# All layer-norm factor steps on GpSimd, two tiles projected in float32, and a rearranged start, in a fused attention and MLP-mixer kernel

## The chip, the cores and the metric

The kernel runs on one core of a Trainium2 chip. The time is the device time of one execution in microseconds (us). Five engines run beside each other, each with its own list of instructions that it works off in order: TensorE (PE, matmuls, with its weight loads as PEld), VectorE (DVE), ScalarE (ACT), GpSimd (POOL) and SyncE (SP), which here issues every DMA. They wait for each other only through semaphores.

## The reference, cut to what matters

```python
xn = layernorm(x)                                   # 2048 rows of 512, float32
qkv = xn @ wqkv                                     # 512 x 1536; 32 heads of 16
# row s attends to rows s, s-2, ..., s-14 (8 keys, dilation 2); s < 0 masked
o = softmax(q.k * 16**-0.5) @ v;  s = o @ wo
y = layernorm(xn)                                   # a second norm, on the first one's result
h = gelu_tanh(y @ w1 + b1)                          # 512 -> 1376
g = silu(h @ w2 + b2)                               # 1376 -> 512
return x + s * g
```

## The kernel before, in words

**Tiles.** The 2048 rows are split into two classes of 1024 (even and odd rows, `c` = 0 and 1), each in 8 tiles `i` of 128 rows by 512. A unit is one class and one block of 8 heads (`hb` = 0 to 3), so there are 8 units, class 0 first. A unit has its projection (`qkv`: 8 tiles, each 12 matmuls of 384 columns) and its attention (`attention`, nearly all on VectorE). The MLP has 4 chunks of 512 rows and 11 blocks `f` of 128 hidden units; one block is 12 matmuls of 512 columns in `mlp1` and 12 in `mlp2`. The output projection is `wo_first` for class 0 and `wo_last` for class 1.

**Precision.** A float32 operand is held as a float16 half `hi` and a remainder `lo`, and a product is three float16 matmuls (hi hi, lo hi, hi lo). Weights are scaled by a power of two first, which needs the sum of their squares: `prep_q` for `wqkv`, and the blocks around `sumsq` and `split` for `w1`, `w2` and `wo`. A sum of squares runs on ScalarE, is totalled over partitions by a small matmul with the matrix `fours` (`total`), and VectorE works out the scale (`half_exp`, `up`, `down`). ScalarE or VectorE then makes `hi`, and VectorE makes `lo`.

**Layer norm.** `ln0` norms class 0. Per group of tiles: `stats` (mean and variance, VectorE), then `factors`. The two norms are folded into one: `rb` is the factor of the row, `cT` a second one that is put in when the projection is evicted (`cs` is `cT` times the weights' inverse scale). In `factors` the two powers run on GpSimd (L512 for `rb`, L519 for `cT`) and the steps between them on VectorE (L504, L508, L515 to L518). The normed tile `y` is made by VectorE (L564) or, for groups whose first tile is in `ACT_Y`, by ScalarE (`y_act`, L531 and L534). TensorE transposes it (L571), ScalarE casts it to `hi` (L581), VectorE makes `lo` (L582). `ln1` does the same later for class 1, in one group of 8.

**Order.** `Plan` takes all operations with an estimated duration and a priority, and places them one by one; what it places fixes each engine's list. A projection may start when the readers of the buffer `U` that it will be evicted into are placed (`after` in `qkv`). Small rings of buffers (`Ring`) set how far one engine can run ahead: two PSUM banks `ps`, two `mh`, four `z`, two for scores `L`. `WAKE0` and `WAKE` are matmuls on constants (L1044) that keep TensorE busy before there is data.

**Loads.** `LOADS` is the order of the first DMAs: tile 2 of `x`, the two halves of the first `wqkv` block (`"q0"`, `"q2"`), tile 3, then tiles 0 and 1, 4 and 5, 6 and 7 in pairs; after them `w1`, the second `wqkv` block, and `w2`. Groups are normed in the order of `GROUPS`.

Of the kernel before, what the change touches and what calls it, by code (L numbers as in the profile page):

```python
# [18 lines left out]
P = 128  # L19
# [5 lines left out]
NI = 8  # L25
# [52 lines left out]
class Op:  # L78
    __slots__ = ("eng", "dur", "fn", "prio", "table", "bufs", "preds", "succs", "npred",
                 "ready", "nbytes", "n", "port", "rate", "issue", "tail")  # L80


class Plan:
# [9 lines left out]
    def add(self, eng, dur, fn, reads=(), writes=(), prio=None, table=None, nbytes=0,  # L93
            after=None, holds=(), port=False, rate=350e3, issue=0.55, tail=1.4):
# [15 lines left out]
        o.port, o.rate, o.issue, o.tail = port, rate, issue, tail  # L110
# [159 lines left out]
WAKE0 = 22  # L270
# [7 lines left out]

U1MH = 4
# [4 lines left out]
PURG, WURG = 0.14, 0.05  # L284
DVE1 = 1.0417e-3
# [5 lines left out]
def tile_mixer(ctx, tc, a_x, a_wqkv, a_wo, b_w1, b_b1, b_w2, out):  # L291
# [168 lines left out]
    def prep_q(hb):  # L460
        col = R_s.new()
        for k in range(0, KT, 2):
# [5 lines left out]
            act(768, go, [("stq", hb, k)], [(col, k), ("wqh", hb, k), ("wqh", hb, k + 1)],  # L468
# [25 lines left out]
    def factors(n, mv, mk, cdst, ckeys, bias=True, close=None, pp=None, **k):  # L494
# [9 lines left out]
        dve(n, lambda: nc.vector.tensor_scalar(p0b.t[:, 0:n], V(), (1.0 + EPS) / YS ** 2,  # L504
                                               EPS * EPS / YS ** 2, op0=ALU.mult, op1=ALU.add),
            mk, [p0b], **k)
        if bias:
            dve(n, lambda: nc.vector.tensor_scalar(p0b.t[:, 8:8 + n], mv()[:, 0:n, 0], -1.0, None,  # L508
                                                   op0=ALU.mult), mk, [(p0b, 1)], **k)
        if close:  # L510
            close()
        pool(0.42 + 0.14 * n, lambda: nc.gpsimd.tensor_tensor(  # L512
            rb.t[:, 0:n], p0b.t[:, 0:n], halves[:, 0:n], op=ALU.pow), [p0b], [(rb, 0)], prio=pp, port=False)
        with pl.fuse():
            dve(n, lambda: nc.vector.tensor_scalar(a0(), V(), EPS, None, op0=ALU.add), mk, [(A, 0)])  # L515
            dve(n, lambda: nc.vector.reciprocal(a1(), a0()), [(A, 0)], [(A, 1)])
            dve(n, lambda: nc.vector.tensor_tensor(a1(), a1(), V(), op=ALU.mult), [(A, 1)] + mk, [(A, 1)])
            dve(n, lambda: nc.vector.tensor_scalar(a1(), a1(), EPS, None, op0=ALU.add), [(A, 1)], [(A, 1)])  # L518
        pool(0.42 + 0.14 * n, lambda: nc.gpsimd.tensor_tensor(  # L519
            cdst, a1(), halves[:, 8:8 + n], op=ALU.pow), [(A, 1)], ckeys, port=False)  # L520
        return rb, p0b
# [6 lines left out]
    def y_act(x, rb, a, keys, y, *ykey):  # L528
        rb, p0b = rb
        with pl.fuse("act"):  # L530
            act(1, lambda: nc.scalar.activation(rb.t[:, 8 + a:9 + a], p0b.t[:, 8 + a:9 + a], AF.Identity,  # L531
                                                scale=rb.t[:, a:a + 1]),
                [(rb, 0), (p0b, 1)], [(rb, 1, a)])
            act(512, lambda: nc.scalar.activation(  # L534
                y(), x(), AF.Identity, bias=rb.t[:, 8 + a:9 + a], scale=rb.t[:, a:a + 1]),
                keys + [(rb, 0), (rb, 1, a)], list(ykey), aps=2)
# [701 lines left out]
```

## Time and profile before

| | |
|---|---|
| median of 3 executions | 424.58 us (423.83 to 424.82) |
| the profiled execution | 423.72 us, of which the span of the profile is 421.9 us |
| TensorE busy | 410.7 us (97%) |
| VectorE busy | 392.1 us (93%) |
| ScalarE busy | 216.0 us (51%) |
| GpSimd busy | 78.9 us (19%) |
| granted TensorE clock, mean | 0.99 of full speed |

A row of the timeline gives start, duration, engine, line of the kernel, operation, `out<-in` by tile names with shapes, a count of like instructions in a row, and in brackets the idle time before it with what ended it. A row of a table by stage gives, for a stretch of time, its length, the busy time of each engine with the number of instructions, the granted clock of TensorE, the share of the DMA engines and their rate. In a row of grouped instructions stand count, busy time, mean of one in ns, and the idle time before.

### The profile page before, as it was taken

How to read it: one execution, taken by the hardware profiler on the slowest of the kernel's cores; microseconds unless marked ns; L12 is line 12 of the kernel's file. 1: busy time of each engine (PE TensorE's matmuls, PEld its weight loads, DVE VectorE, ACT ScalarE, POOL GpSimd, SP SyncE). 2: the span in 40 equal slices, each digit the busy share in tenths (PEclk: the TensorE clock that was granted, in tenths of full speed). 3: DMA queues.
4: the chain of work that ended last, by engine and by line, in shares of the span. 5: the costliest groups of instructions: out<-in, count | busy, mean ns of one | idle time of the engine just before them, and what ended most of it. 6: DMA issues, size and time to landing. Idle time of an engine off the chain costs nothing.

```text
span 421.9 us, 5568 instructions
## 1 busy us (share of the span) xinstructions
PE 410.7 (97%) x2111; PEld 209.8 (50%) x2111; DVE 392.1 (93%) x402; ACT 216.0 (51%) x325; POOL 78.9 (19%) x119
## 2 busy tenths in 40 slices
PE   6899999999999999999999999999999999999995
PEld 4466544445644464446545644554445544444442
DVE  5967999999999999899999999999999999999953
ACT  5699984862478553942565361325122664263500
POOL 4310200001451052003400520052003400520031
PEclk8899999999999999999999999999999999999999
DMA  8964260120044047440362051114434344016132
GB/s 302 414 225 138 62 224 2 63 88 0 6 123 159 2 100 187 100 98 3 91 170 76 2 140 47 46 54 138 149 110 91 94 101 143 2 38 211 26 124 99
DMA packets 42650, 44.83 MB, mean 106 GB/s; under 512 B 27480, under 2 KB 27920, under 8 KB 42112
## 3 DMA queue, kind: packets, MB, share of 16 engines
q1 hardware_dynamic: 42624, 44.49, 34.7%
q8 instruction: 16, 0.26, 0.3%
q14 instruction: 10, 0.08, 0.1%
HBM read 23.53 MB, written 7.34 MB: 73 GB/s over the span
## 4 chain that ended last, share of the span: by engine, by line
DVE 46%; PE 39%; issue 8%; DMA 3%; POOL 2%; SPq 1%; ACT 1%; DVEq 0%; ACTq 0%
DVE prod L691 10%; PE z L945 10%; PE ps L632 9%; PE mh L900 9%; DVE L L694 8%; DVE prod L747 6%; DVE prod L742 5%; PE ps L817 5%; DVE h L923 2%; PE z L817 2%; PE mh L632 2%; POOL prod L771 2%; DVE w L437 2%; DVE bn L525 2%; DVE wq L485 1%
## 5 line engine op out<-in xcount | busy, mean ns | idle before, releaser
L900 PE MATMUL mh<-yT,w 128*128 128x512 f16 (+1 forms) x528 | 121.3, 379 | 0.7 <-ACT h L932 0.5
L632 PE MATMUL ps<-wq,yT 128*128 128x384 f16 x696 | 117.8, 328 | 0.5 <-DVE f L831 0.5
L945 PE MATMUL z<-w,h 128*128 128x512 f16 x480 | 111.6, 379 | 0.0
L632 PEld LDWEIGHTS <-yT 128*128 128x128 f16 x768 | 75.7, 99 | 51.5 <-issue 2.4
L900 PEld LDWEIGHTS <-w 128*128 128x128 f16 (+1 forms) x528 | 52.9, 100 | 61.8 <-issue 1.2
L945 PEld LDWEIGHTS <-h 128*128 128x128 f16 x480 | 47.0, 98 | 55.2
L691 DVE TENSOR_TENSOR prod<-U 128x2048 f32<-128x2048 f32 x32 | 73.1, 2291 | 1.3 <-DMA U<-U 0.2
L917 ACT ACTIVATE mh<-mh,b1T,hsc 128x512 f32<-128x512 f32 (+1 forms) x44 | 33.0, 749 | 79.9 <-PE mh L900 73.4
L694 DVE TENSOR_REDUCE L<-prod 128x128 f32<-128x2048 f32 x32 | 72.8, 2282 | 0.4
L648 ACT ACTIVATE U<-ps,cs 128x384 f32<-128x384 f32 x58 | 33.6, 579 | 67.6 <-PE ps L632 62.8
L747 DVE TENSOR_TENSOR prod<-L,U 128x2048 f32<-128x2048 f32 x28 | 63.4, 2284 | 0.2
L770 POOL COPY gate<-prod 1x1 f32<-1x1 f32 x21 | 4.4, 210 | 236.4 <-DVE prod L691 204.7
L742 DVE TENSOR_TENSOR prod<-prod,prod 128x2048 f32<-128x2048 f32 x16 | 36.5, 2281 | 0.0
L771 POOL TENSOR_TENSOR prod<-prod 128x1024 f32<-128x1024 f32 x14 | 32.9, 2351 | 0.0
L817 PEld LDWEIGHTS <-oT 128*128 128x128 f16 x189 | 18.5, 98 | 22.1
L920 ACT ACTIVATE h<-mh,hsc 128x512 f16<-128x512 f32 x40 | 27.4, 686 | 0.9
L817 PE MATMUL ps<-wo,oT 128*128 128x512 f16 x120 | 27.0, 379 | 0.0
L923 DVE SCALAR_TENSOR_TENSOR h<-mh,hsc,h 128x512 f16<-128x512 f32 x32 | 23.8, 743 | 1.1 <-ACT h L920 1.1
L730 ACT ACTIVATE o<-prod,osc 128x1024 f16<-128x1024 f32 (+1 forms) x9 | 9.5, 1052 | 15.1 <-POOL prod L771 10.5
L771 POOL TENSOR_TENSOR prod<-prod,prod 128x1024 f32<-128x1024 f32 x7 | 16.4, 2349 | 0.0
L917 ACT ACT_TABLE_LOAD x11 | 14.1, 1283 | 0.2
L632 PE MATMUL mh<-wq,yT 128*128 128x384 f16 x72 | 13.4, 330 | 0.0
(151 smaller groups left out, 340.5 us busy)
## 6 DMA issues: line engine op xcount, KB each, us to landing
f<-in_A_x_dram SPq DMA_DIRECT2D x31, 256.0 KB, 3.5
U<-U SPq DMA_DIRECT2D x16, 392.0 KB, 3.8
gd<-f SPq DMA_DIRECT2D x12, 256.0 KB, 2.0
oT<-in_B_w_dram SPq DMA_DIRECT2D x2, 1024.0 KB, 10.3
yT<-in_B_w_dram SPq DMA_DIRECT2D x2, 1024.0 KB, 12.8
f<-gd SPq DMA_DIRECT2D x8, 256.0 KB, 3.1
out_dram<-f SPq DMA_DIRECT2D x8, 256.0 KB, 2.0
out_dram<-U SPq DMA_DIRECT2D x7, 256.0 KB, 2.0
```

Of the source, the lines that this page charges most:

```text
L632: nc.tensor.matmul(b.t[:, 0:384], y[:, s, k, o:o + P], wq[:, hb, t, k], start=(n == 0), stop=(n == 11))
L648: act(384, lambda i=i, b=b: nc.scalar.activation(U3[:, i:i + 31:15, :], b.t[:, 0:384].rearrange("p (t e) -> p t e", t=3), AF.Identity, sca ...
L691: dve(2048, lambda p2=p2, g=g: nc.vector.tensor_tensor(p2(), q, slots(Ut, KH, 2 * g), op=ALU.mult), qk + [("kh", ub, 0), ("kh", ub, 1), (" ...
L694: dve(2048, lambda pr=pr, g=g: nc.vector.tensor_reduce(L3()[:, 2 * g:2 * g + 2], pr.t.rearrange("p (r f d) -> p r f d", r=2, d=DH), AX.X, ...
L742: dve(n, lambda: nc.vector.tensor_tensor(d(), a(), b(), op=ALU.add), keys, [dkey])
L747: dve(2048, lambda: nc.vector.tensor_tensor(pr.t.rearrange("p (r f d) -> p r f d", r=2, d=DH), L3()[:, 2 * g:2 * g + 2].rearrange("p r (f ...
L771: nc.gpsimd.tensor_tensor(x.t[:, 0:1024], x.t[:, 0:1024], y(), op=ALU.add)
L817: nc.tensor.matmul(b.t, oT[:, hb, i // 4, s, i % 4], wo[:, t, hb], start=(hb == 0 and n == 0), stop=(hb == last and n == 2))
L900: nc.tensor.matmul(b.t[0:M], w1[:, s, k, f * P:f * P + M], yT[ch][:, t, k], start=(n == 0), stop=(n == 11))
L917: act(512, lambda: nc.scalar.activation(b.t[0:M], b.t[0:M], AF.Gelu_apprx_tanh, bias=b1T[0:M, f:f + 1], scale=hsc[0:M, 1:2]), [b, ("b1T",) ...
L923: dve(512, lambda: nc.vector.scalar_tensor_tensor(lo()[0:M], b.t[0:M], hsc[0:M, 2:3], hi()[0:M], op0=ALU.mult, op1=ALU.subtract), [b, hk], ...
L945: nc.tensor.matmul(z.t, hl[s][0:K, t * P:(t + 1) * P], w2[0:K, w, f], start=(f == 0 and n == 0), stop=(f == NF - 1 and n == 2))
```

## The change

- `factors` runs wholly on GpSimd. The reciprocal of VectorE is gone: `cT` is now YS^-1 (var + eps)^-0.5 times `p0b` times `rb`. The bias of a tile that ScalarE norms (minus mean times factor) is made there too, one step per tile, and the small ScalarE step (L531) is gone. `cs` of unit 0 is made on GpSimd.
- Tiles 0 and 1 are normed singly, and tile 0's `y` is made on VectorE (`ACT_Y` without 0).
- Tiles 2 and 3 (`FP`) are projected for unit 0 in float32: ScalarE copies the transposed tile to SBUF in float32, TensorE multiplies it by the loaded, unscaled `wqkv` in 4 matmuls of 384 columns. Their float16 halves, which the later units and the MLP read, are made later than tile 1's (`later`).
- `LOADS` puts tile 3 between the two halves of the first `wqkv` block and loads tiles 0 and 1 by two DMAs. `prep_q(0)` gets a lower priority and is added after the first group.
- Four more matmuls on constants (`WAKE0`).
- For units 2 to 7 only the first tile's projection waits for the readers of `U`, for all of q, k and v, and is planned 3 us later (`QSLACK`); the other tiles wait only for a PSUM bank.
- Blocks 2 and 3 of the first MLP chunk use the `ps` banks (`AHEAD`); ScalarE makes the halves of `h` in the order of the blocks.
- The ring `lw` has 24 buffers for 8.

```diff
-GROUPS = [(2,), (3,), (0, 1), (4, 5), (6, 7)]
-LOADS = [(2, 1), "q0", "q2", (3, 1), (0, 2), (4, 2), (6, 2)]
-FP = ()
-ACT_Y = (0, 1, 4, 5)
+GROUPS = [(2,), (3,), (0,), (1,), (4, 5), (6, 7)]
+LOADS = [(2, 1), "q0", (3, 1), "q2", (0, 1), (1, 1), (4, 2), (6, 2)]
+FP = (2, 3)
+ACT_Y = (1, 4, 5)
...
-WAKE0 = 22
+WAKE0 = 26
+AHEAD = (2, 3)
+PQ0 = 0.35
+QSLACK = 3.0
...
     def factors(n, mv, mk, cdst, ckeys, bias=True, pp=None):
-        dve(n, lambda: nc.vector.tensor_scalar(p0b.t[:, 0:n], V(), (1.0 + EPS) / YS ** 2,
-                                               EPS * EPS / YS ** 2, op0=ALU.mult, op1=ALU.add),
-            mk, [p0b], **k)
+        small, power = 0.21, 0.42 + 0.14 * n
+        pool(small, lambda: nc.gpsimd.tensor_scalar(
+            p0b.t[:, 0:n], V(), (1.0 + EPS) / YS ** 2, EPS * EPS / YS ** 2, op0=ALU.mult, op1=ALU.add),
+            mk, [p0b], prio=pp, port=False)
+        pool(power, lambda: nc.gpsimd.tensor_tensor(
+            rb.t[:, 0:n], p0b.t[:, 0:n], halves[:, 0:n], op=ALU.pow), [p0b], [(rb, 0)], prio=pp, port=False)
         if bias:
-            dve(n, lambda: nc.vector.tensor_scalar(p0b.t[:, 8:8 + n], mv()[:, 0:n, 0], -1.0, None,
-                                                   op0=ALU.mult), mk, [(p0b, 1)], **k)
+            for a in range(n):
+                pool(small, lambda a=a: nc.gpsimd.tensor_scalar(
+                    rb.t[:, 8 + a:9 + a], mv()[:, a:a + 1, 0], rb.t[:, a:a + 1], -1.0, op0=ALU.mult, op1=ALU.mult),
+                    [mk[a], (rb, 0)], [(rb, 1, a)], prio=pp, port=False)
-        with pl.fuse():
-            dve(n, lambda: nc.vector.tensor_scalar(a0(), V(), EPS, None, op0=ALU.add), mk, [(A, 0)])
-            dve(n, lambda: nc.vector.reciprocal(a1(), a0()), [(A, 0)], [(A, 1)])
-            dve(n, lambda: nc.vector.tensor_tensor(a1(), a1(), V(), op=ALU.mult), [(A, 1)] + mk, [(A, 1)])
-            dve(n, lambda: nc.vector.tensor_scalar(a1(), a1(), EPS, None, op0=ALU.add), [(A, 1)], [(A, 1)])
-        pool(0.42 + 0.14 * n, lambda: nc.gpsimd.tensor_tensor(
-            cdst, a1(), halves[:, 8:8 + n], op=ALU.pow), [(A, 1)], ckeys, port=False)
+        pool(small, lambda: nc.gpsimd.tensor_scalar(
+            a0(), V(), EPS, YS ** -2, op0=ALU.add, op1=ALU.mult), mk, [(A, 0)], port=False)
+        pool(power, lambda: nc.gpsimd.tensor_tensor(a0(), a0(), halves[:, 0:n], op=ALU.pow),
+             [(A, 0)], [(A, 0)], port=False)
+        pool(small, lambda: nc.gpsimd.tensor_tensor(
+            a1(), p0b.t[:, 0:n], rb.t[:, 0:n], op=ALU.mult), [p0b, (rb, 0)], [(A, 1)], port=False)
+        pool(small, lambda: nc.gpsimd.tensor_tensor(cdst, a0(), a1(), op=ALU.mult), [(A, 0), (A, 1)], ckeys, port=False)
...
     def y_act(x, rb, a, keys, y, *ykey):
-        with pl.fuse("act"):
-            act(1, lambda: nc.scalar.activation(rb.t[:, 8 + a:9 + a], p0b.t[:, 8 + a:9 + a], AF.Identity,
-                                                scale=rb.t[:, a:a + 1]),
-                [(rb, 0), (p0b, 1)], [(rb, 1, a)])
...
     def ln0(ii, xs, xkeys):
-                yf = yF[i] = R_L.new()
+                yf = yF[i] = (R_L if i in (2, 3) else R_f).new()
...
+            (later.append if i in FP else apply)(halves16)
...
     def qkv(c, hb, u):
-                   after=pl.users([b] + [("v", ub, i)]))
+                   after=pl.users([b] + [(x, ub, j) for x in "qkv" for j in range(NI)] if n == 0 else [b]),
+                   slack=QSLACK if u > 1 and n == 0 else 0.0)
...
     def mlp1(ch, f):
-        b = R_mh.new()
+        b = (R_ps if ch == 0 and f in AHEAD else R_mh).new()
...
-                                                  scale=hsc[0:M, 2:3]), [b], [hk])
+                                                  scale=hsc[0:M, 2:3]),
+                [b] + [("hseq", NF * ch + f - 1)] * (NF * ch + f > 0), [hk, ("hseq", NF * ch + f)])
...
-    pl.prio = 0.05
-    prep_q(0)
     pl.prio = 0.1
     for p in groups:
+        if p == groups[1]:
+            with prio(PQ0):
+                prep_q(0)
         pl.prio += 0.1
         ln0(p, [xk[i][0] for i in p], [xk[i][1] for i in p])
+    for f in later:
+        f()
```

In the planned lists this moves the following. VectorE has 37 instructions fewer: 32 small ones less before the MLP, one `y` more, and 6 small ones less in `ln1`. ScalarE has 12 of L531 less, one `y` less and two float32 copies more. GpSimd has 2 powers and 45 small steps more. On TensorE 24 float16 matmuls of 384 columns become 8 in float32, and 4 on constants are added. TensorE's list now has the transposes of tiles 3, 0 and 1 between the float32 matmuls of tiles 2 and 3, and the total of `prep_q(0)` behind the transposes of tile 3. In the units 2 and 3 two tiles of the projection come earlier, among MLP blocks. In `wo_last` the first three head blocks of tiles 0 to 3 (36 matmuls) all come before the fourth block of tile 0.

More of the change, by code (lines that the diff above doesn't have):

```diff
@@ L79 @@
     __slots__ = ("eng", "dur", "fn", "prio", "table", "bufs", "preds", "succs", "npred",
-                 "ready", "nbytes", "n", "port", "rate", "issue", "tail")
+                 "ready", "nbytes", "n", "port", "rate", "issue", "tail", "slack")
 class Plan:
@@ L196, in done @@
             m = margin.get(s.eng, 0.0) if s.eng != o.eng else -LAT["pe"] if o.eng == "pe" else 0.0
-            s.ready = max(s.ready, end + m)
+            s.ready = max(s.ready, end + m + (s.slack if margin else 0.0))
             s.npred -= 1
```

56 lines of the change are left out of this document (27 added, 29 removed).

## The prediction

> **What bounds the kernel now.** I read the busy shares of the profile's page first, then the table by stage, then the timelines of the first 50 us.
>
> ```profile
> span 421.9 us, 5568 instructions
> PE 410.7 (97%) x2111; PEld 209.8 (50%) x2111; DVE 392.1 (93%) x402; ACT 216.0 (51%) x325; POOL 78.9 (19%) x119
> DVE 46%; PE 39%; issue 8%; DMA 3%; POOL 2%; SPq 1%; ACT 1%; DVEq 0%; ACTq 0%
> ```
> ```profile
> 7.20:10.60 3.40, 2.23 (x10) 1.48 (x10) 3.16 (x15) 2.07 (x4) 0.77 (x2) 0.50 1.06 400
> 10.60:14.10 3.50, 3.50 (x14) 1.76 (x13) 3.36 (x11) 0.65 (x2) 0.66 (x2) 0.52 1.02 428
> 14.10:17.50 3.40, 2.52 (x17) 1.51 (x16) 3.12 (x15) 2.88 (x7) 2.75 (x4) 1.00 1.00 399
> 0.00:25.00 25.00, 19.42 (x108) 12.46 (x109) 19.39 (x69) 16.37 (x32) 10.03 (x22) 0.86 0.93 364
> 25.00:36.00 11.00, 11.00 (x72) 6.86 (x71) 4.89 (x13) 10.57 (x18) 0.00 (x0) 1.00 0.23 77
> 36.00:100.00 64.00, 63.34 (x324) 31.66 (x323) 63.40 (x76) 47.62 (x78) 3.19 (x7) 1.00 0.28 95
> 100.00:275.00 175.00, 174.87 (x911) 89.59 (x910) 172.04 (x140) 90.11 (x132) 36.63 (x52) 1.00 0.31 83
> 275.00:397.00 122.00, 121.58 (x605) 59.80 (x605) 119.60 (x91) 50.09 (x66) 23.96 (x36) 1.00 0.34 96
> ```
> The columns after the length are PE, PEld, DVE, ACT, POOL, granted clock. From 36 to 397 us TensorE idles for 0.66 + 0.13 + 0.42 = 1.2 us and VectorE for 0.6 + 2.96 + 2.4 = 6.0 us: both are full, and neither alone is the bound. What can move the end is how early both become full. Before 25 us TensorE is fed late and has half its clock from 7.2 to 14.1 us; before 36 us VectorE idles 6.1 us behind ScalarE.
>
> ```profile
> 10.93 2.77 PE L632 MATMUL ps<-wq,yT 128*128 128x384 f16 x8
> 20.54 1.09 PE L571 MATMUL z<-ident,f 128*128 128x128 f32 x8 [0.50 <-DVE yT L582]
> 24.46 0.81 PE L632 MATMUL mh<-wq,yT 128*128 128x384 f16 x4
> 27.85 2.11 PE L632 MATMUL mh<-wq,yT 128*128 128x384 f16 x12
> 29.80 2.11 PE L632 MATMUL ps<-wq,yT 128*128 128x384 f16 x12
> 49.91 4.70 PE L900 MATMUL mh<-yT,w 128*128 128x512 f16 x21
> ```
> A projection tile at full clock takes 1.95 us (27.85 to 29.80), a matmul of it 0.1625, so one of 512 columns about 0.217; at half clock eight took 2.6 or 0.32 each. From 24.46 us TensorE runs without a gap to the MLP's start at 49.91: that is 25.45 us, 152 matmuls at 0.1625 (24.7) and small ones. Units 0 and 1 have 192, so only 40 were done by 24.46.
>
> **The change, part by part: the start.**
>
> ```profile
> 5.28 0.55 DVE L564 TENSOR_SCALAR f<-prod,lw,lw 128x512 f32<-128x512 f32 x1
> 6.89 0.69 DVE L525 BATCH_NORM_STATS2 bn<-prod 128x6 f32<-128x512 f32 x1 [1.07 <-DMA prod<-in_A_x_dram]
> 14.52 0.29 ACT L531 ACTIVATE lw<-lw,lw 128x1 f32<-128x1 f32 x1 [3.18 <-DVE lw L526]
> 22.32 1.00 DVE L564 TENSOR_SCALAR f<-prod,lw,lw 128x512 f32<-128x512 f32 x2
> 25.15 1.91 ACT L383 ACTIVATE w<-oT 128x2048 bf16<-128x2048 f32 x1
> 35.97 0.16 DVE L400 TENSOR_REDUCE s<-z 128x1 f32<-128x4 f32 x1 [2.73 <-PE z L396]
> ```
> ```profile
> L770 POOL COPY gate<-prod 1x1 f32<-1x1 f32 x21 | 4.4, 210 | 236.4 <-DVE prod L691 204.7 <-DVE osc L415 31.7
> L512 POOL TENSOR_TENSOR lw<-lw,halves 128x1 f32<-128x1 f32 x2 | 1.1, 556 | 2.9 <-DVE ssq L402 2.2 <-DVE lw L515 0.7
> L512 POOL TENSOR_TENSOR lw<-lw,halves 128x8 f32<-128x8 f32 x1 | 1.7, 1652 | 3.8 <-DVE lw L508 3.8
> L519 POOL TENSOR_TENSOR cT<-lw,halves 128x8 f32<-128x8 f32 x1 | 2.8, 2785 | 0.0
> L534 ACT ACTIVATE f<-prod,lw 128x512 f32<-128x512 f32 x4 | 3.3, 813 | 0.1
> L581 ACT CAST yT<-z 128x512 f16<-128x512 f32 x8 | 4.6, 583 | 0.6 <-DVE cs L617 0.4
> L516 DVE RECIPROCAL lw<-lw 128x2 f32<-128x2 f32 x3 | 0.5, 165 | 0.1
> ```
> *GpSimd.* No small arithmetic step on GpSimd is shown. Its nearest row is the copy of one element, 0.21 us; the ends are 0.1 (half that copy) and 0.56 (a power on one column). I take 0.21, since the steps are as small and have no power in them. A single tile's row factor is then two steps and a power, 0.21 + 0.21 + 0.56 = 1.0 us, where now one VectorE step of about 0.15 and the power stand before `y`. That costs 0.25 us on tile 2 (`y` at 5.5 for 5.28). The 33 small steps and two more powers before the MLP, 33 x 0.21 + 2 x 0.56 = 8 us, lie on an engine that is idle 15 of the first 25 us.
>
> *VectorE* loses 32 steps before the MLP. At the reciprocal's 0.165 that is 5.3 us (2.6 if half of each overlaps its neighbour) and it gains one `y` of 0.55; net about -4. VectorE is busy 19.4 of 25 us, so this is on the path to the later tiles.
>
> *Loads.* Tile 3 now passes the second half of `wqkv`. Its statistics waited 1.07 us for the DMA until 6.89; now they follow tile 2's `y`, at 6.1. The extra DMA is one more issue on SP's queue, ahead of `w1`, which has slack. Tile 3's `y`: 6.1 + 0.69 + 0.18 + 1.1 (GpSimd) = 8.05.
>
> *The weight scale* becomes later. The total stands behind tile 3's transposes, and VectorE does `y` of tile 3 and the statistics of tiles 0 and 1 first: 8.05 + 0.55 + 2 x 0.85 + 4 x 0.15 = 10.95 us. Float32 is its cover: two tiles don't need the scale.
>
> *TensorE.* A float32 matmul of 384 columns isn't in the trace. From below: a float32 transpose of 128 columns took 1.09/8 = 0.136 us, three of them 0.41. From above: four times the float16 matmul, 0.65. I take 0.65, for the reason that an upper end is safe here; eight are 5.2 us for 3.9 of 24 float16 ones, so 1.3 us more work, in time when TensorE stood. The first can start after transposes and copy at about 7.6 us, not 10.93. With three transposes (1.65) and the total (0.3) between them they end at 7.6 + 7.15 = 14.75, if the clock is full. The Trainium skill ("FP8 and Floating Point Precision", TensorE Precision Notes) says that true float32 takes four passes through the array; by that the upper end holds, and by the transposes' row the eight would take 3.3 us and free TensorE 1.9 us sooner.
>
> *ScalarE.* After the scale at 11.0 it does four weight halves (0.53 each start to start), one eviction (0.47), one cast (0.53), one `y` (0.72): 14.9. Left before the first square sum of `w1` are one eviction, seven casts, two `y`, two evictions and two sums of 0.82, together 0.47 + 3.7 + 1.44 + 0.94 + 1.64 = 8.2: it starts at 23.1, not 25.15. The gain of 2.05 comes from the 3.18 us that it waited until 14.52, and four L531 less.
>
> So at about 20 us tiles 2, 3, 0 and 1 are projected (14.75 + two transposes + 3.9), and with the sums of the second weight block ending at 22 us some 56 of the 192 matmuls' worth are done at 22.9. The other 136 take 22.1 + 0.7, so the MLP starts at 45.7: **a lead of 4.2 us on TensorE**. `hsc`, from which VectorE splits `w1`, follows ScalarE: **a lead of 2.05 us on VectorE**, which is full from there.
>
> ```profile
> 46.44 1.27 DVE L437 SCALAR_TENSOR_TENSOR w<-o,hsc,w 128x1024 f16<-128x1024 f32 x1
> ```
> The MLP's first block needs the first three of `w1`'s four pieces. The third's remainder ended at 46.44 + 1.27 = 47.7, with VectorE's lead 45.7; the block's last three matmuls want it at 45.7 + 9 x 0.217 = 47.6. So `w1` doesn't hold TensorE, with 1.9 us to spare. What is late next is ScalarE's evictions of unit 1, each planned one step earlier between the square sums.
>
> **The rest.** In `ln1` VectorE loses six steps.
>
> ```profile
> 123.16 0.16 DVE L504 TENSOR_SCALAR lw<-mv 128x8 f32<-128x8 f32 x1
> 124.02 2.29 DVE L691 TENSOR_TENSOR prod<-U 128x2048 f32<-128x2048 f32 x1
> ```
> They take 124.02 - 123.16 = 0.86 us of a full engine: VectorE's lead becomes 2.9. The ScalarE steps dropped there are covered. `AHEAD`, the order of `h`'s halves and the new `after` only reorder TensorE's list; with 1.2 us of idle to win after 36 us I put them at nothing, ends -1 and +1.5, since two tiles now hold both `ps` banks until `U` is free.
>
> At the end TensorE's larger lead must not meet late attention:
> ```profile
> 400.56 0.75 DVE L732 SCALAR_TENSOR_TENSOR o<-prod,osc,o 128x512 f16<-128x512 f32 x1 [0.79 <-ACT o L730]
> 406.97 9.88 PE L817 MATMUL z<-wo,oT 128*128 128x512 f16 x45
> DMA to landing us min/median/max: 3.1/3.1/3.1
> ```
> The last half of the attention is ready at 400.56 + 0.75, lands 3.1 us later at 404.5, and is needed after nine matmuls at 408.9: 4.4 us of slack, more than the two leads differ by. The first half gets 18 more matmuls of cover by the new order.
>
> **Sum.** The end moves by VectorE's 2.9 at the least and TensorE's 4.2 at the most; I take the middle, 3.6. The profiled execution took 423.72 for its span of 421.9, so 420.1; it stands 0.86 under the median of 424.58. Against the median: **421.0 us**.
>
> **Rivals.**
> *The lead is lost on the way* (17%): an engine's list fits less well, TensorE idles 2 to 3 us more in the middle at the held `ps` banks. For it: both engines have nothing to spare. Against it: 0.13 us of idle in 175. It gives 423.0 to 424.5.
>
> *Slower by the clock* (12%): the float32 matmuls stand ahead of the transposes of tiles 0 and 1. The clock was half from 7.2 to 14.1. If it is again, the 7.15 us from 7.6 become 10.4 (6.5 us yield 3.25); ScalarE's lead turns into -1.2, and with `ln1`'s 0.86 the time is 424.9. If it stays half until 17.5, 1.7 more: 426.6. Half clock beyond 14.1 us decides. Against it: TensorE has four more constant matmuls, and float32 work in the stretch where it stood.
>
> *GpSimd becomes the start's bound* (15%): a power on eight columns took 1.65 us, the next one 2.79 beside L691, a two-input VectorE step from 124.02: 1.13 more. If each group's chain of steps slips by 1 us beside VectorE, four in series give 4 us, the last tiles' `y` come at 23.5 for 22.32 and ScalarE's lead is gone: -0.86 + 1.2 makes 424.9; with 0.56 per small step instead of 0.21 some 428. The Trainium skill ("SBUF — State Buffer", Who interferes with whom) says that GpSimd shares a port pair with VectorE under an exclusive lock, held for a whole instruction, and two-input VectorE steps contend; the two rows agree. What would decide is a small step above about 0.4 us.
>
> **Chances.** 0.2% (0.85 us) is about what a measurement of this kernel can tell from no change. The forecast has 56%. Of the rivals' chances I put 14, 0 and 0 to faster, 1, 5 and 4 to the same, and 2, 7 and 11 to slower: faster 70%, same 10%, slower 20%. The range: below, TensorE's lead and all idle, 4.2 + 1.2 = 5.4, 419.2; above, where the slower cases begin, 425.4.
>
> **What would show it.** Right: first float32 matmul near 7.6 us, L383's first start near 23, MLP start near 46, `w1` split near 34, a flat 100 to 275. Wrong: small GpSimd steps over 0.4 us, half clock past 14 us, idle TensorE after 50 us, or the attention as the last wait at the end.

## The result, and the profile after

The changed kernel takes 421.86 us (median of 4 runs, 421.53 to 422.0), the kernel before beside it 424.4 (423.83 to 424.82): a ratio of 0.994, 95% interval 0.9923 to 0.9957, or 2.5 us less. Forecast were 421.0 and 3.6 us; the interval puts the gain at 1.8 to 3.3 us, so less was gained than forecast. The profiled execution took 421.77 us for a span of 420.0, 1.95 less than that of before.

The page of the changed kernel: span, busy times of the engines, and the shares by engine of the chain that ended last.

```profile
span 420.0 us, 5549 instructions
PE 410.1 (98%) x2107; PEld 209.5 (50%) x2107; DVE 387.7 (92%) x365; ACT 211.6 (50%) x314; POOL 91.8 (22%) x166
PE 78%; DVE 10%; POOL 3%; issue 3%; DMA 2%; ACT 1%; SPq 0%; DVEq 0%; POOLq 0%; ACTq 0%
```

VectorE is 4.4 us less busy, GpSimd 12.9 more. The chain now runs through TensorE for 78% (39% before) and through VectorE for 10% (46%). The table by stage of the changed kernel (columns as before: length, PE, PEld, DVE, ACT, POOL, granted clock, DMA):

```profile
7.20:10.60 3.40, 3.38 (x18) 2.25 (x17) 2.29 (x7) 2.53 (x6) 2.70 (x10) 1.00 1.07 414
10.60:14.10 3.50, 3.50 (x15) 2.08 (x14) 3.40 (x10) 3.08 (x6) 3.06 (x10) 1.00 1.02 426
0.00:25.00 25.00, 21.34 (x123) 14.17 (x124) 15.78 (x41) 16.81 (x31) 19.26 (x57) 1.00 0.95 362
36.00:100.00 64.00, 64.00 (x327) 31.73 (x325) 62.74 (x74) 46.47 (x79) 3.20 (x7) 1.00 0.25 85
100.00:275.00 175.00, 173.57 (x907) 89.19 (x906) 171.35 (x130) 88.76 (x126) 40.77 (x64) 1.00 0.30 76
275.00:397.00 122.00, 121.88 (x602) 59.22 (x600) 118.05 (x91) 48.03 (x63) 23.51 (x35) 1.00 0.36 106
```

The clock is full from 7.2 to 14.1 us, where it was 0.50 and 0.52. From 36 to 100 us TensorE has no gap (0.66 us before); from 100 to 275 it idles 1.43 us, where it had 0.13. The rows of the changed kernel's timelines that answer to those shown of before:

```profile
5.61 0.55 DVE L571 TENSOR_SCALAR f<-prod,lw,lw 128x512 f32<-128x512 f32 x1 [1.33 <-POOL lw L517]
7.54 1.56 PE L651 MATMUL ps<-prod,L 128*128 128x384 f32 x4
12.20 2.10 PE L651 MATMUL mh<-prod,L 128*128 128x384 f32 x6
16.78 1.52 ACT L539 ACTIVATE f<-prod,lw 128x512 f32<-128x512 f32 x2 [0.89 <-POOL lw L521]
21.39 1.00 DVE L571 TENSOR_SCALAR f<-prod,lw,lw 128x512 f32<-128x512 f32 x2 [0.88 <-POOL lw L517]
22.00 0.66 PE L578 MATMUL z<-ident,f 128*128 128x128 f32 x4 [0.85 <-DVE f L571]
23.05 0.66 PE L578 MATMUL z<-ident,f 128*128 128x128 f32 x4 [0.28 <-DVE yT L592]
24.23 1.91 ACT L392 ACTIVATE w<-oT 128x2048 bf16<-128x2048 f32 x1
47.04 3.19 PE L914 MATMUL mh<-yT,w 128*128 128x512 f16 x14
56.68 4.49 DVE L704 TENSOR_TENSOR prod<-U 128x2048 f32<-128x2048 f32 x2
134.61 0.81 PE L961 MATMUL z<-w,h 128*128 128x512 f16 x3 [0.23 <-ACT f L977]
135.77 2.10 PE L961 MATMUL z<-w,h 128*128 128x512 f16 x9 [0.35 <-ACT f L977]
190.58 9.75 PE L644 MATMUL ps<-wq,yT 128*128 128x384 f16 x59 [0.85 <-ACT U L661]
414.48 0.82 PE L880 MATMUL z<-wo,oT 128*128 128x256 f16 x6
```

A float32 matmul leaves two records, so the row at 7.54 is two matmuls and that at 12.20 three. The MLP starts at 47.04 us, 2.87 earlier (49.91). The three idles with a releaser behind it sum to 1.43 us. The last group of matmuls, which in the kernel before stood at

```profile
416.69 0.82 PE L867 MATMUL z<-wo,oT 128*128 128x256 f16 x6
```

starts 2.21 us earlier. From the start of the MLP to that group TensorE idles for 1.09 us before (0.54 and 0.55) and 1.43 after; without these idles the stretch is 365.69 us before (416.69 - 49.91 - 1.09) and 366.01 after. So the end is the MLP's start plus some 365.7 us plus what TensorE idles behind it; a tail of 5.1 to 5.6 us, from the start of that group to the end of the span, follows in every kernel. This sum was then made for every kernel that ran (times in us; "idle" is TensorE's behind the MLP's start; "rest" is last group less start less idle; start, idle and last group belong to the profiled execution):

| kernel | MLP start | idle | last group | rest | profiled | median |
|---|---|---|---|---|---|---|
| before | 49.91 | 1.09 | 416.69 | 365.69 | 423.72 | 424.4 |
| changed | 47.04 | 1.43 | 414.48 | 366.01 | 421.77 | 421.86 |
| e1 no float32 | 47.39 | 0.73 | 413.85 | 365.73 | 421.12 | 422.04 |
| e2 factors on VectorE | 47.47 | 0.63 | 413.39 | 365.29 | 420.36 | 420.17 |
| e3 old start condition | 47.59 | 2.44 | 415.52 | 365.49 | 422.92 | 422.92 |
| e4 no `AHEAD`, no order of `h` | 46.98 | 5.76 | 420.12 | 367.38 | 427.4 | 427.5 |
| f1 `ln1` on VectorE | 47.14 | 0 | 412.61 | 365.47 | 419.81 | 419.86 |
| f2 = e4 with `ln1` on VectorE | 47.27 | 2.05 | 415.29 | 365.97 | 422.49 | 421.92 |
| f3 = e1 and e2 | 49.87 | 0.24 | 415.33 | 365.22 | 422.33 | 422.06 |
| f4 before, with the later parts | 49.83 | 1.64 | 417.60 | 366.13 | 424.63 | 425.2 |
| g1 old loads and groups | 47.81 | 4.82 | 419.52 | 366.89 | 426.79 | 429.11 |
| g2 best | 46.26 | 0 | 411.74 | 365.48 | 418.71 | 418.39 |
| g3 planned cost of `ln1` | 47.29 | 1.20 | 414.06 | 365.57 | 421.34 | 421.37 |
| h1 fewer constant matmuls | 47.41 | 0 | 412.86 | 365.45 | 420.07 | 419.99 |

The rest is 365.2 to 366.1 in all but e4 and g1, where the matmuls behind the long idle ran more slowly (e4: 12 took 4.44 us for 2.75 elsewhere, at a granted clock of 0.62; g1: 24 took 5.74 for 3.94, at 0.54 from 168.3 to 172.0 us): 1.7 and 1.8 us, which bring them to 365.7 and 365.1.

### The profile page after: what moved, and what is told of

Same layout as the page of the kernel before. It is cut to its first block, busy times and chain, and to the rows that moved or that the text cites. A ratio compares the mean times of both kernels' runs of the same rounds, so it can differ in the third digit from the quotient of the medians.

```text
span 420.0 us, 5549 instructions
## 1 busy us (share of the span) xinstructions
PE 410.1 (98%) x2107; PEld 209.5 (50%) x2107; DVE 387.7 (92%) x365; ACT 211.6 (50%) x314; POOL 91.8 (22%) x166
## 4 chain that ended last, share of the span: by engine, by line
PE 78%; DVE 10%; POOL 3%; issue 3%; DMA 2%; ACT 1%; SPq 0%; DVEq 0%; POOLq 0%; ACTq 0%
PE ps L644 22%; PE z L961 22%; PE mh L914 21%; PE ps L830 6%; PE z L830 2%; DVE prod L704 2%; PE mh L644 2%; DVE prod L760 2%; DVE L L707 2%; PE mh L830 1%; PE ps L914 1%; DMA U<-U 1%; DVE f L614 1%; POOL lw L517 1%; DMA f<-in_A_x_dram 1%
## 5 line engine op out<-in xcount | busy, mean ns | idle before, releaser
L914 PE MATMUL mh<-yT,w 128*128 128x512 f16 (+1 forms) x504 | 115.5, 379 | 0.1
L644 PE MATMUL ps<-wq,yT 128*128 128x384 f16 x684 | 114.5, 326 | 0.9 <-ACT U L661 0.8
L644 PEld LDWEIGHTS <-yT 128*128 128x128 f16 x744 | 72.7, 98 | 49.5 <-issue 1.1
L704 DVE TENSOR_TENSOR prod<-U 128x2048 f32<-128x2048 f32 x32 | 73.1, 2290 | 1.6 <-DMA U<-U 0.6
L931 ACT ACTIVATE mh<-mh,b1T,hsc 128x512 f32<-128x512 f32 (+1 forms) x42 | 31.4, 749 | 81.5 <-PE mh L914 81.4
L784 POOL TENSOR_TENSOR prod<-prod 128x1024 f32<-128x1024 f32 x14 | 32.9, 2349 | 0.0
L935 ACT ACTIVATE h<-mh,hsc 128x512 f16<-128x512 f32 x38 | 26.0, 684 | 0.8
L784 POOL TENSOR_TENSOR prod<-prod,prod 128x1024 f32<-128x1024 f32 x7 | 16.4, 2347 | 0.0
L931 ACT ACT_TABLE_LOAD x11 | 14.1, 1283 | 0.2
L823 POOL TENSOR_TENSOR U<-U,f 128x512 f32<-128x512 f32 x4 | 5.1, 1268 | 33.5 <-DVE U L893 33.5
```

The costliest lines, as they stand in the source:

```text
L644: nc.tensor.matmul(b.t[:, 0:384], y[:, s, k, o:o + P], wq[:, hb, t, k], start=(n == 0), stop=(n == 11))
L704: dve(2048, lambda p2=p2, g=g: nc.vector.tensor_tensor(p2(), q, slots(Ut, KH, 2 * g), op=ALU.mult), qk + [("kh", ub, 0), ("kh", ub, 1), (" ...
L784: nc.gpsimd.tensor_tensor(x.t[:, 0:1024], x.t[:, 0:1024], y(), op=ALU.add)
L914: nc.tensor.matmul(b.t[0:M], w1[:, s, k, f * P:f * P + M], yT[ch][:, t, k], start=(n == 0), stop=(n == 11))
L931: act(512, lambda: nc.scalar.activation(b.t[0:M], b.t[0:M], AF.Gelu_apprx_tanh, bias=b1T[0:M, f:f + 1], scale=hsc[0:M, 1:2]), [b, ("b1T",) ...
L935: act(512, lambda: nc.scalar.activation(hi()[0:M], b.t[0:M], AF.Identity, scale=hsc[0:M, 2:3]), [b] + [("hseq", NF * ch + f - 1)] * (NF * ...
```

## The experiments

The kernel before, run beside each group, took 423.89 us (e), 424.17 (f), 424.19 (g) and 424.04 (h); each ratio is to these. Between groups the kernel before itself differs by up to 0.5 us (423.89 to 424.4), so a difference of that size between two medians of different groups is not clear of the noise.

**e1: without float32.** With it `prep_q(0)` goes back ahead of the first group.

```diff
-FP = (2, 3)
+FP = ()
...
+    pl.prio = 0.05
+    prep_q(0)
```

> The changed kernel with tiles 2 and 3 projected in float16 like the others (FP empty) and the first weight block's scale prepared first, as before. Theory 1 (the gain is made at the start, mainly because TensorE gets work it can do before the weight scale is there): first projection matmul at 10.5 us or later for 7.54, the clock half again between 7 and 14 us, the MLP's start back at 48.5 to 50 us for 47.04, time 423.3 to 424.5 us. Theory 2 (the gain comes from the small steps that left VectorE): MLP's start at most 47.5, time at most 422.4. Theory 3 (the gain comes from the new order of the projections and MLP steps after the start): time at most 422.4 whatever the MLP's start is.

Measured: 422.04 us, ratio 0.9959 (0.9935 to 0.9982). The changed kernel's own median is only 0.2 lower, and the MLP starts at 47.39, so Theory 1's price for float32 falls; Theories 2 and 3 both allow this result. But the six times lie in two groups that go with the mean granted clock of the execution: 420.76 to 421.12 at 0.995 to 0.997, 422.96 to 423.38 at 0.990 to 0.992. The changed kernel has 0.998 to 1.0 in its four. This points to the clock: float32 gives TensorE work early, with which the clock stays full. In the executions without float32 whose clock is low for a shorter time, e1 is even 0.7 to 1.1 us faster than the changed kernel's median. This is not shown by itself: of the three executions with the lower clock there is no trace.

**e2: all factor steps on VectorE, float32 kept.**

```diff
-        pool(small, lambda: nc.gpsimd.tensor_scalar(
-            p0b.t[:, 0:n], V(), (1.0 + EPS) / YS ** 2, EPS * EPS / YS ** 2, op0=ALU.mult, op1=ALU.add),
+        dve(n, lambda: nc.vector.tensor_scalar(p0b.t[:, 0:n], V(), (1.0 + EPS) / YS ** 2,
+                                               EPS * EPS / YS ** 2, op0=ALU.mult, op1=ALU.add),
...
```

> The changed kernel with the factor steps on VectorE and only the powers on GpSimd, as before, the small ScalarE steps included; float32 and all else stay. Theory 1 (start, mainly float32): float32 starts at about 7.4 us, VectorE busy 18 us or more of the first 25 for 15.8, MLP's start 47 to 48.2, time 421.8 to 423. Theory 2 (the steps that left VectorE): MLP's start 49 or later, time 423.7 or more. Theory 3 (order after the start): time as the changed kernel, 421.5 to 422.2.

Measured: 420.17 us, ratio 0.9911 (0.9896 to 0.9926). No theory's range holds this time, only Theory 1's range for the MLP's start (47.47). It is faster than the changed kernel by 1.7, so Theory 2 falls: GpSimd's factor steps cost time. That is not in `ln0`: the MLP starts 0.43 later than in the changed kernel. The idle at 134 to 136 us and at 190 is gone.

**e3: the old start condition of the projections, without the 3 us.**

```diff
-                   after=pl.users([b] + [(x, ub, j) for x in "qkv" for j in range(NI)] if n == 0 else [b]),
-                   slack=QSLACK if u > 1 and n == 0 else 0.0)
+                   after=pl.users([b] + [("v", ub, i)]))
```

> The changed kernel with the old condition for a projection's start (every tile waits for the readers of v of its buffer, no 3 us more). Theories 1 and 2 (gain at the start): MLP's start 47.0 as in the changed kernel, time 421.2 to 422.5. Theory 3 (order after the start): MLP's start 47.0 too, but TensorE idles 1.5 us more than the changed kernel between 50 and 400, time 423.3 or more.

Measured: 422.92 us, ratio 0.9976 (0.9966 to 0.9986): 1.06 more than the changed kernel, and in no theory's range. In the profiled executions TensorE's idle is 1.0 longer (2.44 for 1.43), the start 0.55 later and the rest 0.5 shorter. On e3's page all this idle stands in one row, and its cause in the next:

```profile
L913 PE MATMUL mh<-yT,w 128*128 128x512 f16 (+1 forms) x504 | 115.5, 379 | 2.4 <-DVE h L938 2.4
L938 DVE SCALAR_TENSOR_TENSOR h<-mh,hsc,h 128x512 f16<-128x512 f32 x32 | 23.6, 741 | 2.6 <-ACT h L934 2.6
```

The waits lie at 132.74 us (1.79) and 141.32 (0.65). Ahead of the first, ScalarE waits 1.96 us for GpSimd's last step of `ln1`, until 130.45, with the half of `h` behind it at 131.23. At 190 us there is no idle. So most of e3's idle comes with `ln1`'s chain, on which e4 says more; what the start condition is worth without that chain, no run shows.

**e4: without `AHEAD` and without the forced order of `h`'s halves.**

```diff
-AHEAD = (2, 3)
+AHEAD = ()
...
-                [b] + [("hseq", NF * ch + f - 1)] * (NF * ch + f > 0), [hk, ("hseq", NF * ch + f)])
+                [b], [hk])
```

> The changed kernel with all MLP blocks in the mh banks and the halves of h without the forced order. Theories 1 and 2 (gain at the start): MLP's start 47.0, time 421.5 to 422.6, at most 0.7 us lost between blocks 1 and 3 where ScalarE is full. Theory 3 (order after the start): 423 or more.

Measured: 427.5 us, ratio 1.01 (1.0074 to 1.0126), 5.6 more than the changed kernel. The time is Theory 3's, but the rows of the largest idle tell something else (e4's timelines of ScalarE, GpSimd, VectorE and TensorE):

```profile
129.79 2.24 POOL L530 TENSOR_TENSOR cT<-lw 128x8 f32<-128x8 f32 x1
132.06 0.87 ACT L627 ACTIVATE cs<-cT,qsc 128x8 f32<-128x8 f32 x4 [7.05 <-POOL cT L530]
135.03 0.69 ACT L935 ACTIVATE h<-mh,hsc 128x512 f16<-128x512 f32 x1
135.75 0.75 DVE L939 SCALAR_TENSOR_TENSOR h<-mh,hsc,h 128x512 f16<-128x512 f32 x1 [3.78 <-ACT h L935]
136.56 4.44 PE L914 MATMUL mh<-yT,w 128*128 128x512 f16 x12 [3.65 <-DVE h L939]
```

ScalarE stood 7.05 us for the last GpSimd step of `ln1`. Behind it in ScalarE's list stood the gelu and the half of the next MLP block; VectorE waited for that half, and TensorE for the bank. The same row of the changed kernel, and its GpSimd steps ahead of it:

```profile
121.72 3.67 POOL L517 TENSOR_TENSOR lw<-lw,halves 128x8 f32<-128x8 f32 x1
125.37 1.80 POOL L526 TENSOR_TENSOR lw<-lw,halves 128x8 f32<-128x8 f32 x1
127.25 1.90 POOL L521 TENSOR_SCALAR lw<-mv,lw 128x1 f32<-128x1 f32 x8
129.62 0.87 ACT L627 ACTIVATE cs<-cT,qsc 128x8 f32<-128x8 f32 x4 [2.30 <-POOL cT L530]
```

The chain took from 121.16 to 129.6 us. The plan has it at 5.6 (two powers of 1.54, twelve small steps of 0.21). The Trainium skill ("TensorE: Matmul & The Clock Gate", Architectural detail) says that ScalarE and VectorE work off their queues strictly in order; by that one late operand holds all that is listed behind it, and these rows agree. This is Theory A of the runs that follow.

**f1: only `ln1`'s factor steps back on VectorE.** `factors_dve` is the old form of `factors`; the small ScalarE step of each tile comes back with it.

```diff
-        rb = factors(NI, lambda: mv1, mk, cT[:, 1, :], [("c", 1, i) for i in range(NI)])
+        rb, p0b = factors_dve(NI, lambda: mv1, mk, cT[:, 1, :], [("c", 1, i) for i in range(NI)])
```

> Edit: the changed kernel, with the factor steps of ln1 alone put back on VectorE (its two powers stay on GpSimd); ln0's stay on GpSimd. Theory A (after its start the MLP needs 365.7 us of TensorE work and whatever TensorE idles; GpSimd's long chain for ln1, 121.2 to 129.6 us, is what makes it idle near 134 us): the MLP starts at 47.0 as in the changed kernel, the 0.58 us of idle at 134 to 136 go, other idles may move by up to 0.9; 420.4 to 421.4. Theory B (ln1's steps were a gain, because VectorE was full there): VectorE's six steps come back, 0.86 us, and the time is 422.4 to 422.9.

Measured: 419.86 us, ratio 0.9907 (0.9891 to 0.9924): 2.0 less than the changed kernel, 0.5 beyond Theory A's range. TensorE has no idle left behind the MLP's start. ScalarE still waits for GpSimd, for as long, but it is through with `cs` at 129.1 us for 130.5. The table load ahead of ScalarE's gelu (ACT_TABLE_LOAD, 1.28 us), which stands behind that wait in the changed kernel (130.51), stands ahead of it here (123.71). So the eviction that TensorE waited for at 134 us comes at 131.61 for 133.87:

```profile
124.56 3.62 POOL L550 TENSOR_TENSOR cT<-lw,halves 128x8 f32<-128x8 f32 x1 [0.56 <-DVE lw L549]
128.22 0.88 ACT L652 ACTIVATE cs<-cT,qsc 128x8 f32<-128x8 f32 x4 [2.46 <-POOL cT L550]
```

**f2: e4 with `ln1`'s factor steps on VectorE** (f1's edit on e4).

> Edit: the kernel without AHEAD and without the forced order of h's halves (which took 427.5), with ln1's factor steps back on VectorE besides. Theory A (the 3.65 us of TensorE idle and the half clock behind it in that kernel come from ScalarE waiting 7.05 us for GpSimd's last step of ln1, with the MLP's evictions queued behind the waiting step): both go and the time falls by about 5, to 421.5 to 423.5. Theory B (the banks and the order of the halves are themselves worth 5.7 us): it stays at 426.5 to 428.

Measured: 421.92 us, ratio 0.9955 (0.9937 to 0.9973): 5.6 less than e4, as Theory A has it. So e4's 427.5 stand over f1's 419.86 by 5.6 us of `ln1`'s chain in that list and by 421.92 - 419.86 = 2.06 us of `AHEAD` and the order of `h`. The 2.06 go with f2's idle of 2.05, where f1 has none:

```profile
54.06 1.46 PE L939 MATMUL mh<-yT,w 128*128 128x512 f16 x6 [1.23 <-ACT h L973]
175.13 2.75 PE L939 MATMUL mh<-yT,w 128*128 128x512 f16 x12 [0.42 <-DVE h L964]
189.93 10.23 PE L669 MATMUL ps<-wq,yT 128*128 128x384 f16 x62 [0.40 <-ACT U L686]
```

**f3: e1 and e2 together.** The edits of both.

> Edit: the changed kernel without float32 and with all factor steps back on VectorE: what is left of the change is tiles 0 and 1 normed singly, the loads, four constant matmuls, the banks, the order of h and the start condition. Theory A (each of float32 and GpSimd alone cost or gained little because the lead comes from tile 3's earlier load, the single norms and the clock): the MLP starts at 47.0 to 48.0 and the time is 419.5 to 421.0. Theory C (either of the two is enough for the lead, and without both it is lost): the MLP starts at 49.5 to 50.2 and the time is 423.0 to 424.5.

Measured: 422.06 us, ratio 0.9939 (0.9916 to 0.9961). The profiled execution is Theory C's in its start, 49.87 us. Again the times go with the clock: 420.65 and 420.75 at 0.995, 422.06 to 422.33 at 0.990. The table by stage of that execution:

```profile
10.60:14.10 3.50, 3.23 (x14) 1.89 (x13) 3.41 (x12) 2.29 (x5) 1.60 (x2) 0.50 1.00 419
14.10:17.50 3.40, 3.40 (x17) 1.96 (x16) 3.26 (x11) 1.11 (x2) 0.95 (x2) 0.68 1.01 404
```

The clock is half into the time when TensorE is already full; the 1.5 us between the two groups of times go with that, though only this one execution has a trace. The total is right for neither theory: against the changed kernel's profile the start is 2.83 later, but the idle 1.19 and the rest 0.79 less. Two more pairs can be read from these times. f3 and e2 differ by float32 (and the place of `prep_q(0)`), both with the factors on VectorE: 422.06 and 420.17, so float32 is worth 1.9 us there, where e1 gave 0.2 with the factors on GpSimd. e2 and f1 differ by where `ln0`'s factors run: 420.17 and 419.86, which is within the noise. f3 keeps, besides what was listed before it ran, the longer ring `lw` and two estimates of the plan (0.1 us more for a small step in a fused group, 0.1 for 0.2 for constant matmuls behind the sixteenth); no run takes these alone.

**f4: the kernel before with `AHEAD`, the order of `h` and the start condition alone.** The edits of e3 and e4, made on the kernel before in the other direction.

> Edit: the kernel before with only the later parts of the change: blocks 2 and 3 of the MLP in the ps banks, the order of h's halves, the new start condition with its 3 us. Theory A (these remove idle of TensorE after the MLP's start, of which the kernel before has only 1.1 us): MLP start 49.9, 423.3 to 425.0. Theory B (they are worth 5.7 us by themselves): 418 to 420.

Measured: 425.2 us, ratio 1.0024 (1.0011 to 1.0038), 0.2 above Theory A's range, with the MLP's start at 49.83. Theory B falls. The kernel before had 1.09 us of idle to win; the new order has 1.64, of which 1.45 (0.29 and 1.16) is at held `ps` banks.

**g1: the old loads and groups, float32 and GpSimd kept.**

```diff
-GROUPS = [(2,), (3,), (0,), (1,), (4, 5), (6, 7)]
-LOADS = [(2, 1), "q0", (3, 1), "q2", (0, 1), (1, 1), (4, 2), (6, 2)]
+GROUPS = [(2,), (3,), (0, 1), (4, 5), (6, 7)]
+LOADS = [(2, 1), "q0", "q2", (3, 1), (0, 2), (4, 2), (6, 2)]
...
-ACT_Y = (1, 4, 5)
+ACT_Y = (0, 1, 4, 5)
```

> Edit: the changed kernel with the old GROUPS, LOADS and ACT_Y (tiles 0 and 1 normed and loaded as a pair, tile 0's y on ScalarE, tile 3 behind the second half of the weights); float32 and GpSimd's factor steps stay. Theory A (the lead of 2.9 us in the MLP's start is mostly data: tiles 3, 0 and 1 reach TensorE earlier): the MLP starts at 48.5 to 50 and the time is 423.0 to 425.0. Theory C (the lead is float32's, which fills TensorE before the weight scale is known, or GpSimd's): the MLP starts at 47.0 to 48.0 and the time is 421.3 to 422.5.

Measured: 429.11 us (426.79 to 430.0; the trace is of the fastest), ratio 1.0123 (1.01 to 1.0147). Neither range holds it. The start is Theory C's (47.81: the loads and groups bring 0.77); the rest goes back to `ln1`'s chain, placed by this list beside the projections' evictions (g1's timelines):

```profile
152.69 4.42 DVE L704 TENSOR_TENSOR prod<-U 128x2048 f32<-128x2048 f32 x1 [1.00 <-POOL gate L783]
155.03 3.85 POOL L521 TENSOR_SCALAR lw<-mv,lw 128x1 f32<-128x1 f32 x8
159.35 0.88 ACT L627 ACTIVATE cs<-cT,qsc 128x8 f32<-128x8 f32 x4 [5.63 <-POOL cT L530]
168.30 5.74 PE L644 MATMUL ps<-wq,yT 128*128 128x384 f16 x24 [4.82 <-ACT o L743]
```

The ScalarE step named in the last row is only the nearest in time. These matmuls read the first normed tile of class 1. Its `y` was made at 160.60 us, behind the `cs` that waited for GpSimd; its `lo` at 163.82, behind an L704 that took 4.37 us beside GpSimd's L784; and the DMA that transposes it was issued at 164.78 and had landed at 168.21. A run of g1 with `ln1` on VectorE was not made.

**g2: f1, with the row factor's first step on VectorE and the second factor's first step behind the row's power.**

```diff
-        pool(small, lambda: nc.gpsimd.tensor_scalar(
+        dve(n, lambda: nc.vector.tensor_scalar(
             p0b.t[:, 0:n], V(), (1.0 + EPS) / YS ** 2, EPS * EPS / YS ** 2, op0=ALU.mult, op1=ALU.add),
...
-            a0(), V(), EPS, YS ** -2, op0=ALU.add, op1=ALU.mult), mk, [(A, 0)], port=False)
+            a0(), V(), EPS, YS ** -2, op0=ALU.add, op1=ALU.mult), mk + [(rb, 0)], [(A, 0)], port=False)
```

> Edit: ln1's factor steps on VectorE as in the kernel that took 419.86, and in ln0 the first factor step on VectorE (some 0.15 us) and the first step of the second factor behind the row's power on GpSimd, so that a row's factor waits for one GpSimd step, the power, and not three. Theory A (TensorE has no idle left after the MLP's start, so only the start counts: TensorE waited 1.45 us for y after 16 us): y of tiles 4 to 7 comes 0.5 to 0.8 us earlier, the MLP starts at 46.3 to 46.9, time 419.1 to 419.7. Rival (the lists are planned anew and lose 0.5 to 1.5 us of TensorE after the start): 420.0 to 421.2.

Measured: 418.39 us (418.33 to 418.71), ratio 0.9865 (0.9849 to 0.9882), the fastest of all, 0.7 beyond Theory A's range, with the MLP's start at its edge. The first `y` comes 0.26 earlier than in the changed kernel, the last 0.46, and the MLP starts 0.78 earlier:

```profile
5.35 0.55 DVE L592 TENSOR_SCALAR f<-prod,lw,lw 128x512 f32<-128x512 f32 x1 [0.76 <-POOL lw L517]
20.93 1.00 DVE L592 TENSOR_SCALAR f<-prod,lw,lw 128x512 f32<-128x512 f32 x2
46.26 4.05 PE L939 MATMUL mh<-yT,w 128*128 128x512 f16 x18
```

**g3: the changed kernel, with only the planned durations of `ln1`'s steps changed.** No instruction is added or removed.

```diff
-        small, power = 0.21, 0.42 + 0.14 * n
+        small, power = (0.21, 0.42 + 0.14 * n) if n < NI else (0.25, 2.75)
```

> Edit: the changed kernel, every factor step on GpSimd; only the planned durations of ln1's steps are changed (2.75 us for a power on eight columns, the mean of the 3.67 and 1.80 measured, for 1.54; 0.25 for a small step, for 0.21), so that the plan places what follows them later. No instruction is added or taken away. Theory A (the loss lies in the order: the plan lets ScalarE wait for GpSimd's last step with the MLP's evictions behind it): the 0.58 us of TensorE idle at 134 to 136 go, 420.0 to 421.2. Rival (GpSimd's work itself costs, by its length or by its contention with VectorE): 421.5 to 422.3, as without the edit.

Measured: 421.37 us (421.1 to 421.69), ratio 0.9934 (0.992 to 0.9948), 0.5 less than the changed kernel and between the two ranges. The two intervals overlap, so the time alone decides nothing. The mechanism is shown by the rows: the gelu of the next block now stands ahead of `cs`, ScalarE no longer waits there, and TensorE runs through 134 to 136 us without a gap (g3's timelines):

```profile
129.49 0.75 ACT L931 ACTIVATE mh<-mh,b1T,hsc 128x512 f32<-128x512 f32 x1 [0.61 <-PE mh L914]
130.17 0.86 ACT L627 ACTIVATE cs<-cT,qsc 128x8 f32<-128x8 f32 x4
131.88 5.34 PE L914 MATMUL mh<-yT,w 128*128 128x512 f16 x24
347.37 2.75 PE L914 MATMUL mh<-yT,w 128*128 128x512 f16 x12 [0.57 <-DVE h L939]
```

Of the 2.0 us that f1 wins, this gives at most a quarter: the 0.58 us of idle at 134 to 136 are gone, but an idle of 0.57 comes at 347 us, and 0.63 stays at 190. Which part of the remaining 1.5 us is GpSimd's work itself and which the list, these runs leave open.

**h1: f1 with ten constant matmuls fewer** (`WAKE0` 16 for 26).

> Edit: the kernel that took 419.86 (ln1's factor steps on VectorE, the rest as changed), with ten constant matmuls fewer ahead of the first transposes (WAKE0 16 for 26). Nothing else moves. Theory A (the half clock from 7.2 to 14.1 us followed from TensorE standing before it, and costs only what TensorE's later waits for y don't cover): TensorE stands some 3 us before 6.3, the clock is half again for some 6.8 us in which TensorE would be busy, 3.4 us of work are lost, 1.45 us of later waits cover a part, the MLP starts about 2 us later, near 49.1, 421.5 to 422.3. Rival (the clock doesn't depend on that, or the work before the last y is covered wholly): 419.6 to 420.2.

Measured: 419.99 us (419.55 to 420.79), ratio 0.9907 (0.989 to 0.9923). Theory A's price falls, the rival holds. TensorE did slow down, but for a shorter time, and its waits between 17 and 21 us covered most of it (h1's timeline of TensorE):

```profile
6.34 1.12 PE L599 MATMUL z<-ident,f 128*128 128x128 f32 x4 [1.70 <-DVE f L592]
8.13 2.29 PE L676 MATMUL ps<-prod,L 128*128 128x384 f32 x4
15.89 2.11 PE L669 MATMUL ps<-wq,yT 128*128 128x384 f16 x12
18.49 1.04 PE L599 MATMUL z<-ident,f 128*128 128x128 f32 x8
47.41 2.97 PE L939 MATMUL mh<-yT,w 128*128 128x512 f16 x13
```

The four transposes took 1.12 us for 0.66, the first two float32 matmuls 2.29 for 1.56. The projection at 15.89 is 1.25 us later than in f1 (14.64), the transposes at 18.49, ahead of which f1 waits 0.33, only 0.75 (17.74). From there the delay shrinks to 0.27, by which the MLP starts later than in f1.

## Why the prediction was right, and where only its sum was

The sign and the size were right (2.5 us of the 3.6 forecast, inside the range), and the place was: the start, 2.87 us of it. Which part of the change brings these isn't settled. In the profiled executions going without float32 costs 0.35 of them, the factors on VectorE 0.43, the old loads and groups 0.77; without the first two together 2.83 are gone, in an execution with half the clock from 10.6 to 14.1 us. By the prediction's steps:

- *GpSimd, 0.21 us per small step.* The steps take 0.19 but follow each other at 0.27 to 0.28 (L514 at 4.46, L524 at 4.74, L517 at 5.01), and 0.39 to 0.50 beside some steps of VectorE, one of them 0.86 (L629 at 18.84). The first tile's `y` came at 5.61 for 5.5 forecast, tile 3's at 8.20 for 8.05, the weight scale at 10.84 for 10.95. Not foreseen was the order of the list: a step of the second factor stood ahead of the row's power, and the last group's row factor behind the second factors of the group before. g2 took the first away, with one step to VectorE, and won 1.47 us over f1; the last group's power comes at 19.91 for 20.65, still behind the second factors of the group before. Of the 1.47 us, 0.88 are the MLP's start (46.26 for 47.14).
- *The float32 matmul, 0.65 us.* Three took 12.20 to 14.13, 0.64 each; the first at 7.54 for 7.6; all done at 14.13 for 14.75. The upper end was the right choice: 0.64 is 3.9 times the 0.1625 of float16. The four passes of the Trainium skill's "FP8 and Floating Point Precision" (TensorE Precision Notes) agree. What float32 brings depends on the rest: 0.2 us (e1) or 1.9 (f3 against e2).
- *ScalarE's first square sum of `w1` at 23.1.* It came at 24.23, a lead of 0.92 for 2.05. The term left out ScalarE's waits: 0.89 for GpSimd's bias step at 16.78 and 0.43, 0.72 and 0.39 at other places before 24 us.
- *TensorE's lead of 4.2.* It was 2.87: the sum gave TensorE no wait after 20 us, and it waited 0.85 for the last `y` at 22.00 and 0.28 at 23.05 for a step that makes a `lo`.
- *VectorE's lead as the lower bound of the gain.* This step failed. The split of `w1` began 0.61 us earlier (36.12 for 36.73), the first attention 0.27 (56.68 for 56.95), and the last matmuls 2.21. In all fourteen kernels the end follows TensorE's start and its idles, while the rest (without the slow matmuls of e4 and g1) varies by 1.0 us and the tail by 0.5. "Both are full, and neither alone is the bound" was wrong.
- *`ln1` frees 0.86 us on VectorE.* Wrong in sign: it cost 2.0 us (changed kernel against f1). The step left out who waits behind GpSimd's chain: ScalarE, with the MLP's evictions behind the waiting instruction. In the changed kernel the rows show this for the 0.58 us at 134 to 136; the 0.85 at 190, where an eviction waits for the attention on VectorE, and some 0.5 of the rest differ too, and for these the cause is open.
- *`AHEAD` and the order of `h` at nothing, ends -1 and +1.5.* Wrong: `AHEAD` and the order gained 2.06 us (f1 against f2), beyond the gain's end. The kernel before shows no such idle, and there these parts and the start condition win nothing (f4); that the idle arises only with the new start fits this, but was not tried further. The wrong `ln1` term and this one had opposite signs and nearly cancelled, so that the total came near is in part luck.
- *The tail's slack* held: in the last 23 us TensorE waited for nothing until its last group.

Of the rivals, *the lead is lost on the way* took place in part: 0.85 us of the 1.43 is at held `ps` banks, as it said, and the other 0.58 at a place it didn't name. *Slower by the clock* did not take place; h1, with a shorter slow stretch than it assumed, paid 0.3 us at the MLP's start, where that rival lay 3.9 above the forecast. *GpSimd becomes the start's bound* did not in its size, but its sign did appear, small steps over 0.4 us, and g2 shows that these steps held the start by about 0.8.

## What to carry to other kernels

Where one engine is full to the end, add up its start and its idles, kernel by kernel: a change is worth what it moves in these two. Busy time taken off another full-looking engine was worth nothing by itself here (f1 gives VectorE six steps back and is 2.0 us faster). Parts of a change need not add up: float32 is worth 0.2 or 1.9 us here, by where the factors run. Work moved to an idle engine is not free when an in-order engine waits for it: look at what stands behind the waiting instruction. In a planned kernel the estimate of a moved step is part of the change, since a wrong one (5.6 us for 8.4) puts the wait where it costs.

## What the runs showed of the hardware that was not expected

GpSimd's power on eight columns took 1.66 us in g1 where no step of VectorE with two inputs from SBUF ran, and 3.67 in the changed kernel beside one (L704, from 121.58 to 123.86): 2.0 more, of the 2.1 for which L704 still ran. In g1 VectorE's L704 took 4.42 us for its usual 2.28 while GpSimd's L784 of 2.33 us, started 0.07 earlier, ran:

```profile
149.25 1.66 POOL L517 TENSOR_TENSOR lw<-lw,halves 128x8 f32<-128x8 f32 x1
152.62 2.33 POOL L784 TENSOR_TENSOR prod<-prod 128x1024 f32<-128x1024 f32 x1
```

By these two cases the later one waited for nearly the whole of the earlier one. The Trainium skill ("SBUF — State Buffer", Who interferes with whom) says this of a VectorE instruction with two inputs in SBUF and a GpSimd instruction that reads SBUF; the numbers agree.

In h1 the rows by stage give a granted clock of 1.00 from 5 to 11 us, although the matmuls there took up to 1.7 times as long; the durations are the better witness. In the kernel before, an execution at a mean clock of 1.0 was no faster (423.83 to 424.37) than those at 0.990 to 0.995 (423.21 to 425.56). That TensorE there waits for data in the same stretch and so loses nothing by half the clock is the likely reason; it was not tried by itself.
